# The last store moved behind the branch over the general path, the range check in front of the last sums, and a new order of the work

## The chip, the cores and the metric

The kernel runs on one core of one Trainium2 chip. The metric is the device time of one execution in microseconds (us). TensorE (PE) does the matrix products, VectorE (DVE), ScalarE (ACT) and GpSimd (POOL) the element-wise work, and SyncE (SP) issues nearly all DMAs. Each engine runs its own list of instructions in order and waits on semaphores that the others raise.

## The reference

```python
# q, k, v, a_re, a_im: (batch 4, head 8, seq 768, dim 48)
scale = minimum(mag, 0.999) / (mag + 1e-06)          # mag = |a|
for t in range(S):                                   # complex state S of 48 x 48, per batch and head
    S_re, S_im = a_re_n*S_re - a_im_n*S_im + k_t v_t^T, a_re_n*S_im + a_im_n*S_re
    y[:, :, t] = q_t . S_re
x = y as (4, 768, 384)
h = gelu_tanh(x @ w_in)                              # w_in 384 x 1024
u, v = h[..., :512], h[..., 512:]
v_n = layer_norm(v) * g_ln
v_s = einsum('ts,bsd->btd', w_sg, v_n) + b_sg        # w_sg 768 x 768, along the sequence
out = x + (u * v_s) @ w_out                          # w_out 512 x 384
```

## The kernel before, in words

The program has two paths. The fast path computes the recurrence in chunks of 128 steps by matrix products; it needs the gates (a_re, a_im) and the weights to lie in a range. The general path (`general()`) does the recurrence step by step and is right for any input. The kernel always runs the fast path, gathers on the way the extremes of the gates and weights into `stats`, and at the end branches: if one number, `oki`, says that all 128 partitions were in range, the general path is jumped over; otherwise it runs and writes the output anew. With the inputs timed here it is always jumped over.

The fast path consists of some hundred generators ("chains"), each with a `yield` after every small step: `l`, `g`, `e`, `t`, `p`, `s` (gates: load, logarithms, scale, angles, sine and cosine, by unit of the sequence), `v`, `r`, `z`, `a` (by group of 128 steps: load v, rotate q and k, transpose heads into `Q`, `K` and `kbuf`, attend), `n` (the v half of h, layer norm), `x` (the u half of h), `y` (`spatial()`: v_s, product with u, w_out, sum with x, store), `w` (weights split into a high and a low part, since each product is done as three), `h` and `k` (`gate_range`, `weight_range`), `f` (filler matmuls), `ok` (`check()`). A hand-written string `ORDER` names a chain per token and steps it as often as the token says. A quote mark behind a token sends an element-wise step to POOL or DVE in place of ACT or DVE (`evac`, `high`, `low`, `ew`) and adds filler matmuls in some steps. So the order of instructions on every engine, and in part which engine does a step, is exactly the order of this string.

The end matters here. `y3_0` is the last chain of sums. For its last of four blocks f, PE computes `pvs` (L241), then the products of the first three blocks with w_out (27 matmuls L802 into `po`), while DVE, ACT and POOL make `tg`, `gh` and `gl` of the last block; then come three times three matmuls for the last block (d = 0, 1, 2), each followed by a sum `x<-po,x` on DVE (L832) and a store of 192 KB (L834). The stores of d = 0 and 1 are issued by SP, that of d = 2 by ACT:

```python
(nc.scalar if final and d == NK - 1 else nc.sync).dma_start(out=out[b, ds, tsl], in_=x[:, d, :])
```

The first `ok` step, `in_range()`, stands behind the sums: eight small DVE operations (L844, L845) compare the extremes with their limits, three (L847) multiply the answers, one matmul `pok` (L851) adds them over the partitions, and a cast (L853) writes `oki`. The second `ok` step loads that word into a register of all five engines (TENSOR_LOAD, L964). Then every engine compares and branches (L993). On the path that jumps, each engine raises the semaphores by what the skipped instructions would have raised them: in the built program one step each on ACT, POOL, PE and DVE, and eight in a row on SP, one for each DMA semaphore (named DMAHW0 to DMAHW7 in the program). The end block (L1034) waits on SP for the DMA semaphores, and then all engines meet.

Of the kernel before, what the change touches and what calls it, by code (L numbers as in the profile page):

```python
# [14 lines left out]
ALU = mybir.AluOpType  # L15
# [17 lines left out]
f l0:2 w0 g0:2 g0'' g0:2 w0 g0'' f:2' f f' l1 g1 w0 g0:2 w13 w0 l1 w13:2 t0 m0 e0 w13 w13' w13 p0 g1 e0 p0'' p0:2 s0  # L33
l2 g1:2 e0 g1 w2:3 g1 w2 f m0 e0 e0'' g2 g1:2 w1:4 w1'' w1 e1' l2 s0:2 r0:2'' w6 w6'' v0 t1 p1 g2 e1 g2 p1'' z0' w6'
z0 z0' o0 z0:2 z0' e0 w3 p1 w2'' e0 w3:2 w2 g2 m1 a0 m1 g2 z0 s1 z0' g2 e1:2 e1'' l3 s1:2 e1 t2 g2 p1 g2:4 a0:7 w4 e2
w3 w3'' r1' r1'' v1 w4 l3 m2 o0 w4 e2 w4 g3:2 z1:2 e2 z1 z1' p2 w7 p2' p2 m2 e1 e2'' z1 e2 z1:2 z1' e2:2 a1:2 g3' g3:2
# [4 lines left out]
w5'' z4 v4 n0_0:3 a3 n0_0 z4:5 a4' g5 z4 a4 v5 g5'' r5' z5' z5 g4 z5 w10 w10' a4 p4 m4 z5 m4 w11 a4:3 g5 e4 p4 a4'' p4
l6:2 w10 a4 a4' g5 w14 a4 v6 e4'' e4 n0_0 s4:3 n0_0' z5 z5' z5:2 r6'' w11:2' n0_0 a5' a5 o0 w15 a5:2 n0_0 e4:2 r6 r6'
t5 p5 r6 p5 r6'' n0_0 a5' a5:2 p5 e4 e4' n0_3 g6 x0_0 n0_0 n0_0' x0_0:3 r6 r6'' r6 g5 n0_0'' z6 n0_0'' l8 x0_0 n0_0:2
n0_0' z6 x0_0 z6 x0_0 w15 n0_3 w14 n0_3'' w14 g5 z6 w15 w14 p5 o1 w15 g5 n0_0:2 w14 w14'' n0_3'' g5 n0_3 v7 m5:2 n0_3
x0_0 n0_3 a6 n0_3 a7:2 n0_3:2 a7 w15 w15' p5 a6 n0_3:2 a6:3 a6'' a6 g6 p5 a6'' a6:2 e5 a7'' a7 e5'' n0_3 g6' a6 a7 v8
a7 s5 a7'' a7 e5 n0_3' a6'' e5 a6 a7 n0_3' e5 n0_3 a7 n0_3'' n0_3' n0_3 n0_3'' s5 a7 s5 f r8'' r8 n0_3 n0_3'' g6 x0_3
y0_0 t6 g6 r8'' r8:3 a7 y0_0:3 y0_0' g6 y0_0:2 g6 y0_0 r8 g6:2 p6:3 x0_3:2 y0_0'' x0_3:2 l7:2 x0_3 r8 x0_3 g7:2 y0_0'
# [990 lines left out]
```

## Time and profile before

| | |
|---|---|
| time, median of 3 runs | 434.57 us (433.83 to 434.8) |
| the profiled execution's own time | 435.87 us |
| its span, first to last instruction | 434.2 us, so 1.67 us lie around it |
| mean granted clock of TensorE | 0.992 of full speed |
| busy in the span | PE 96%, DVE 84%, ACT 68%, POOL 29% |
| DMA | 92.95 MB, 214 GB/s |

Busy time is the time in which an engine executes; PE's contains the filler matmuls. The profiled execution is 1.3 us above the median of the runs. A row names a line of the kernel (L241 is line 241), the engine, the operation and the tiles, output first.

### The profile page before, as it was taken

To read this page: it belongs to the slowest core of one execution; us is meant where nothing else is said; L and a number is where in the kernel's file an instruction comes from. 1 tells how busy PE (TensorE), PEld (TensorE's weight loads), DVE (VectorE), ACT (ScalarE), POOL (GpSimd) and SP (SyncE) were. 2 spreads that over 40 slices of the span, in tenths; PEclk is the share of its full clock that TensorE was granted. 3 is DMA by queue.
4 is the path that set the end of the run, shared out by engine and by line. 5 is a ranking of instruction groups with operands and counts; after the bars stand their busy time and mean duration, and the time that the engine had idled before them with its cause. 6 is when DMAs were issued, how large, how long until landed. Compare 5 with 4: busy or idle time off the path is not lost.

```text
span 434.2 us, 9896 instructions
## 1 busy us (share of the span) xinstructions
PE 416.0 (96%) x3924; PEld 378.7 (87%) x3924; DVE 366.8 (84%) x610; ACT 293.2 (68%) x399; POOL 124.1 (29%) x175
## 2 busy tenths in 40 slices
PE   7689999899999999999999999899999999999994
PEld 4367687797999999898999999889999998899994
DVE  5999998998999999988999899887998674768475
ACT  5989999979999497886686862876847223541000
POOL 2047322660602215172112103532131031140010
PEclk9999999989999999999999999999999999999998
DMA  7768675769469988787878985891996956464551
GB/s 222 248 179 246 175 231 136 223 212 286 152 221 246 274 255 258 228 246 231 243 211 253 281 248 166 231 298 47 283 277 226 275 180 200 127 229 125 158 175 59
DMA packets 62940, 92.95 MB, mean 214 GB/s; under 512 B 9892, under 2 KB 44838, under 8 KB 62888
## 3 DMA queue, kind: packets, MB, share of 16 engines
q1 hardware_dynamic: 62744, 92.06, 71.0%
q8 instruction: 32, 0.52, 0.5%
q14 instruction: 20, 0.16, 0.1%
q10 hardware_dynamic: 144, 0.20, 0.1%
HBM read 68.64 MB, written 23.60 MB: 212 GB/s over the span
## 4 chain that ended last, share of the span: by engine, by line
PE 60%; ACT 15%; DVE 12%; DMA 5%; issue 3%; POOL 2%; SPq 1%; DVEq 0%; ACTq 0%
PE pvs L241 20%; PE pu L241 9%; PE pv L241 7%; PE po L802 7%; PE pa L637 5%; ACT L204 4%; PE py L679 3%; PE ps L657 3%; DMA K<-rk 2%; PE py L684 2%; PE pk L622 2%; ACT csn L205 2%; ACT l L205 2%; DMA re<-in_t_re_dram 1%; DVE xl L230 1%
## 5 line engine op out<-in xcount | busy, mean ns | idle before, releaser
L204 ACT ACT_TABLE_LOAD x60 | 77.0, 1283 | 1.9 <-PEq L1023 0.9
L241 PE MATMUL pvs<-wsgh,vh 128*128 128x384 f32 x192 | 65.5, 341 | 0.0
L241 PE MATMUL pvs<-wsgh,vl 128*128 128x384 f32 x192 | 64.7, 337 | 0.0
L241 PE MATMUL pvs<-wsgl,vh 128*128 128x384 f32 x192 | 64.5, 336 | 0.0
L637 PE MATMUL pa<-Q,K 96*64 96x128 f32 (+1 forms) x768 | 40.5, 250 | 1.5 <-DVE K L216 1.4
L637 PEld LDWEIGHTS pa<-Q,K 96*64 96x64 f32 x768 | 36.6, 137 | 5.6 <-issue 3.5
L679 PE MATMUL py<-am,vbuf 128*64 128x128 f32 x384 | 40.4, 281 | 0.1
L241 PEld LDWEIGHTS pvs<-wsgh,vh 128*128 128x128 f32 x192 | 36.0, 188 | 0.6 <-issue 0.4
L241 PEld LDWEIGHTS pvs<-wsgh,vl 128*128 128x128 f32 x192 | 36.0, 188 | 0.3 <-DVE vl L230 0.3
L241 PEld LDWEIGHTS pvs<-wsgl,vh 128*128 128x128 f32 x192 | 36.0, 188 | 0.0
L647 DVE TENSOR_TENSOR am<-pa,mask 128x512 f32<-128x512 f32 x47 | 31.3, 682 | 4.9 <-PE pa L637 4.9
L684 PE MATMUL py<-Q,S 96*48 96x128 f32 x320 | 34.9, 278 | 0.0
L241 PE MATMUL pu<-xh,winh 128*128 128x384 f32 x96 | 33.2, 346 | 0.0
L802 PE MATMUL po<-gh,wouth 128*128 128x384 f32 x96 | 33.0, 343 | 0.0
L241 PE MATMUL pu<-xl,winh 128*128 128x384 f32 x96 | 32.5, 338 | 0.0
L802 PE MATMUL po<-gl,wouth 128*128 128x384 f32 x96 | 32.4, 338 | 0.0
L241 PE MATMUL pu<-xh,winl 128*128 128x384 f32 x96 | 32.4, 337 | 0.0
L802 PE MATMUL po<-gh,woutl 128*128 128x384 f32 x96 | 32.4, 337 | 0.0
L241 PE MATMUL pv<-winh,xh 128*128 128x512 f32 x72 | 29.4, 408 | 0.1
L241 PE MATMUL pv<-winh,xl 128*128 128x512 f32 x72 | 28.6, 398 | 0.9 <-DVE xl L230 0.9
L241 PE MATMUL pv<-winl,xh 128*128 128x512 f32 x72 | 28.4, 394 | 0.0
L679 PEld LDWEIGHTS py<-am,vbuf 128*64 128x64 f32 x384 | 26.5, 138 | 1.5 <-DVE am L647 1.2
(280 smaller groups left out, 1068.3 us busy)
## 6 DMA issues: line engine op xcount, KB each, us to landing
vbuf<-in_t_v_dram SPq DMA_DIRECT2D x24, 288.0 KB, 4.3
K<-rk SPq DMA_DIRECT2D x18, 384.0 KB, 6.2
Q<-rq SPq DMA_DIRECT2D x18, 384.0 KB, 6.4
x<-xd SPq DMA_DIRECT2D x9, 576.0 KB, 4.8
xd<-yp SPq DMA_DIRECT2D x48, 96.0 KB, 3.4
gr<-in_f_im_dram SPq DMA_DIRECT2D x12, 384.0 KB, 4.6
gr<-in_f_re_dram SPq DMA_DIRECT2D x12, 384.0 KB, 4.7
out_dram<-x SPq DMA_DIRECT2D x23, 192.0 KB, 2.5
```

What stands on the lines that cost most here:

```text
L204: nc.scalar.preload_act_table_set(SETS[t])
L205: nc.scalar.activation(out, in_, func, scale=scale, **kw)
L230: ew().tensor_tensor(out=l, in0=src, in1=h.bitcast(F32), op=ALU.subtract)
L241: nc.tensor.matmul(o, w(i), x(i), start=(i == 0 and j == 0), stop=(i == n - 1 and j == 2))
L622: nc.tensor.transpose(pk[:, hh, :], K(4 * g2 + hh), ident[0:2 * D, 0:2 * D])
L637: nc.tensor.matmul(pa[to:to + HC, hh, HC * j:], K(h)[:, HC * j:HC * j + HC], Q(h)[:, HC * j:], start=True, stop=True)
L647: nc.vector.tensor_tensor(out=pairs(am), in0=pairs(pa), in1=upto, op=ALU.mult)
L657: nc.tensor.matmul(ps[r, h, :], kbuf[g % 2][:, h * 2 * D + r.start:h * 2 * D + r.stop], V[:, h * D:(h + 1) * D], start=True, stop=True)
L679: nc.tensor.matmul(py[64 * e:64 * e + 64, p_, :], V[:, at:at + 64], ams[h // 4][:, h % 4, :], start=True, stop=c == 0)
L684: nc.tensor.matmul(py[64 * e:64 * e + D, p_, :], Sb[:, h, :], Q(h), start=False, stop=True)
L802: nc.tensor.matmul(po[d], w[:, f, ds], g[:, f, :], start=f == 0 and j == 0, stop=f == NF - 1 and j == 2)
```

## The change

There are four edits. `ORDER` is written anew as a whole; its last tokens went from `h14:2 y3_0' y3_0 h15 y3_0:8 ok y3_0 ok` to `h14:2 y3_0 y3_3:2 ok y3_0:7 f:2 ok`, so the first `ok` step now comes before the last sums and the second one at the very end. The last of the three sums goes to a tile of its own, `end`, with the tag "u", whose buffers the general path uses as well. Its store is taken out of `spatial()` and stands in `last_store()`, behind the branch. It is still issued by ACT. Line numbers behind the sums shift by 6 to 10: the check is L850 to L859, the load L973, the branch L1002, the last store L968, the end block L1044.

```diff
 ORDER = """
-f l0:2 w0 g0:2 g0'' g0:2 w0 g0'' f:2' f f' l1 g1 w0 g0:2 w13 w0 l1 w13:2 t0 m0 e0 w13 w13' w13 p0 g1 e0 p0'' p0:2 s0
+l0 o0 l0 g0 w0 g0:4 l1 w13 l1 g1 m0 w0:2 g0'' w0 f'' g0:2 w13 o0 w13:2 w13'' w13' t0 e0 g1 e0 m0 p0 p0'' p0:2 s0 g1''
...
 """
@@ spatial
             result(d, range(NF - 1, NF) if final else range(NF))
             yield
+            if final and d == NK - 1:
+                if "end" not in run:
+                    run["end"] = mp.tile([P, MT], F32, tag="u", name="end", bufs=UB)
+                nc.vector.tensor_tensor(out=run["end"], in0=po[d], in1=x[:, d, :], op=ALU.add)
+                yield
+                return
             nc.vector.tensor_tensor(out=x[:, d, :], in0=po[d], in1=x[:, d, :], op=ALU.add)
             yield
-            (nc.scalar if final and d == NK - 1 else nc.sync).dma_start(out=out[b, ds, tsl], in_=x[:, d, :])
+            nc.sync.dma_start(out=out[b, ds, tsl], in_=x[:, d, :])
             yield
@@
+    def last_store():
+        nc.scalar.dma_start(out=out[B - 1, DM - P:DM, UFINAL * P:UFINAL * P + MT], in_=run["end"])
+
@@
     with tc.If(ok[0] < P, label="over"):
         general()
+    last_store()
```

By the order of the built programs PE keeps its 2756 matmuls on the fast path, fillers included. DVE goes from 607 to 595 instructions, ACT from 395 to 399 and POOL from 179 to 184; ACT's table loads go from 60 to 59.

The first place is ACT's list up to `xh` of the block n0_3, the high part of x that the first layer-norm block of the second half of the sequence needs. `yp` is the evacuated attention output, `vr` the normalized v, `inv`, `re` and `l` belong to the gates. Before:

```order
L218 COPY yp<-py 128x512 [waits DMAHW4_49,DMAHW5_49,DMAHW3_49,DMAHW6_49,DVE_49,PE_49]
L204 ACT_TABLE_LOAD
L205 ACTIVATE re_1005<-re_1005 128x768 [waits DMAHW2_49]
L204 ACT_TABLE_LOAD
L205 ACTIVATE u__1181<-pu 128x384 [waits PE_49]
L205 ACTIVATE u__1194<-pu 128x384 [waits PE_49]
L205 ACTIVATE vr<-vr,nt,ny 128x512 [waits DVE_49,Pool_49]
L205 ACTIVATE vh_1217<-vr 128x512 [waits Activation_49]
L205 ACTIVATE vr<-vr,nt,ny 128x512 [waits DVE_49]
L205 ACTIVATE u__1224<-pu 128x384 [waits PE_49]
L205 ACTIVATE xh<-x 128x1152 [waits DMAHW6_49,DMAHW7_49,DMAHW5_49,PE_49]
```

After:

```order
L218 COPY yp<-py 128x512 [waits DMAHW5_49,DMAHW6_49,DVE_49,PE_49]
L204 ACT_TABLE_LOAD
L205 ACTIVATE inv_852<-l_971,cols 128x768 [waits DVE_49]
L205 ACTIVATE re_914<-re_914 128x768 [waits DMAHW1_49]
L204 ACT_TABLE_LOAD
L205 ACTIVATE u__1184<-pu 128x384 [waits PE_49]
L205 ACTIVATE u__1201<-pu 128x384 [waits PE_49]
L205 ACTIVATE vr<-vr,nt,ny 128x512 [waits Pool_49]
L205 ACTIVATE u__1214<-pu 128x384 [waits PE_49]
L205 ACTIVATE vh_1216<-vr 128x512 [waits Activation_49]
L205 ACTIVATE xh<-x 128x1152 [waits DMAHW5_49,DMAHW6_49,DMAHW4_49,PE_49]
```

`inv<-l,cols` has come in front of `xh`, and the second `vr<-vr,nt,ny` has gone behind it.

The second place is the end of DVE's list, where `ok_...` holds the answers of the check and `stats` the extremes. Before, the three sums, then the check:

```order
L395 ISA stats 128x1
L832 TENSOR_TENSOR x<-po,x 128x384 [waits PE_49] x3
L844 TENSOR_REDUCE ok_5176<-stats 128x1
L845 TENSOR_SCALAR ok_5176<-ok_5176 128x1 [waits DVE_49]
L844 TENSOR_REDUCE ok_5176<-stats 128x1
```

After, the end of the check, the cast, and then the sums:

```order
L853 TENSOR_TENSOR ok_5163<-ok_5163 128x1
L853 TENSOR_TENSOR ok_5163<-ok_5163 128x1 [waits DVE_49] x2
L855 MEMSET ones 128x2
L859 CAST oki<-pok 1x2 [waits PE_49]
L838 TENSOR_TENSOR x<-po,x 128x384
L838 TENSOR_TENSOR x<-po,x 128x384 [waits PE_49]
L835 TENSOR_TENSOR end<-po,x 128x384 [waits PE_49]
L973 TENSOR_LOAD oki [waits DVE_49]
L1002 COMPARE_AND_BRANCH
```

The whole check has moved in front of the sums, and between the last sum and the branch only the load is left. On PE, `pok` has moved the same way: it now stands between the matmuls of d = 0 and those of d = 1.

The third place is ACT's end. Before, with the store in front of the load and the branch (the row behind them belongs to the skipped path):

```order
L205 ACTIVATE gh<-tg 128x384 [waits DVE_49,PE_49]
L834 DMA out_dram<-x 128x384 [waits DMAHW5_49,DVE_49]
L964 TENSOR_LOAD oki [waits DVE_49]
L993 COMPARE_AND_BRANCH
L205 ACTIVATE winh<-bits 128x512 [waits DVE_49] x5
```

After, the rows at the end of the skipped path, and the store behind it:

```order
L205 ACTIVATE gh<-tg 128x384 [waits DVE_49] x4
L1002 UNCONDITIONAL_BRANCH
L1002 UNCONDITIONAL_BRANCH [waits Activation_49]
L968 DMA out_dram<-end 128x384 [waits DMAHW7_49,DVE_49]
L1044 UNCONDITIONAL_BRANCH
```

The store now waits for a DMA semaphore, DMAHW7, and for DVE. In the built program the counts it waits for contain what the skipped path would have added: they are reached by the last of SP's eight steps behind the branch and by DVE's step.

## Rows read from the trace of the kernel before

**Rows 1.** Windows: length, busy of PE, PEld, DVE, ACT, POOL; clock, DMA share, GB/s.

```profile
80.00:102.00 22.00, 19.88 (x160) 17.31 (x159) 19.79 (x31) 19.72 (x24) 11.93 (x18) 0.92 0.75 227
102.00:420.00 318.00, 316.40 (x3057) 302.67 (x3058) 268.72 (x441) 200.59 (x271) 83.88 (x107) 1.00 0.74 221
```

**Rows 2.** Waits of PE, 30 to 430 us: total, times, longest.

```profile
PE pa L637 <- DVE K L216: 1.4, 1, 1.4
PE pk L622 <- DMA K<-rk: 1.2, 1, 1.2
```

**Rows 3.** Chain of waits, 80 to 104 us: start, length, what.

```profile
84.04 1.91 DVE k L467
...
86.77 0.58 DVE K L216
...
92.27 0.59 ACT yp L218
```

**Rows 4.** ACT by line and shape, 0 to 104 us: count, busy, mean ns.

```profile
L218 ACT COPY K<-pk 96x512 f32<-96x512 f32 x10 | 5.8, 576 | 0.0
...
L218 ACT COPY Q<-pk 96x512 f32<-96x512 f32 x6 | 3.4, 573 | 0.0
...
L205 ACT ACTIVATE inv<-l,cols 128x768 f32<-128x768 f32 x2 | 1.9, 932 | 0.0
...
L205 ACT ACTIVATE vr<-vr,nt,ny 128x512 f32<-128x512 f32 x2 | 1.6, 809 | 0.0
L205 ACT ACTIVATE vh<-vr 128x512 fp32r<-128x512 f32 x2 | 1.3, 626 | 0.0
```

**Rows 5.** DVE by line and shape, whole span: count, busy, mean ns.

```profile
L467 DVE TENSOR_TENSOR k<-k,em 128x768 f32<-128x768 f32 x9 | 9.6, 1067 | 0.5 <-ACT em L205 0.5
```

**Rows 6.** POOL from 76 to 96 us: start, length, what.

```profile
82.18 2.95 POOL L230 TENSOR_TENSOR wsgl<-raw,wsgh 128x768 fp32r<-128x768 f32 x1
```

**Rows 7.** Timeline from 427 us, all engines: start, length, what.

```profile
427.31 1.61 DVE L832 TENSOR_TENSOR x<-po,x 128x384 f32<-128x384 f32 x3 [1.06 <-PE po L802]
...
427.89 0.87 SPq L834 DMA_DIRECT2D out_dram<-x  x2
...
428.83 0.15 DVE L844 TENSOR_REDUCE ok<-stats 128x1 f32<-128x12 f32 x1
...
430.48 0.19 PE L851 MATMUL pok<-ones,ok 128*1 128x2 f32 x2 [2.15 <-DVE ones L849]
430.70 0.15 DVE L853 CAST oki<-pok 1x2 int32<-1x2 f32 x1 [0.28 <-PE pok L851]
```

**Rows 8.** Line 964, the load of the word to branch on: ns, start.

```profile
L964 SPq TENSOR_LOAD <-oki x1: 467/467/467, 430.9 to 430.9; - x1
```

**Rows 9.** Line 993, the branch: ns, first and last start.

```profile
L993 SPq EVENT_SEMAPHORE  x8: 17/17/17, 432.2 to 432.8; - x8
...
L993 SPq COMPARE_BRANCH  x1: 70/70/70, 431.7 to 431.7; - x1
...
L993 DVEq EVENT_SEMAPHORE  x1: 21/21/21, 432.1 to 432.1; - x1
```

**Rows 10.** Line 1034, the end of the program: ns, first and last start.

```profile
L1034 SPq EVENT_SEMAPHORE  x10: 17/28/28, 432.9 to 434.1; - x10
...
L1034 SPq DRAIN  x3: 7/7/7, 433.4 to 433.7; - x3
```

**Rows 11.** Line 834, all stores of sums: issue to landing.

```profile
DMA to landing us min/median/max: 1.9/2.5/5.5
```

**Rows 12.** Timeline of DVE, 422 to 427 us: start, length, what.

```profile
422.68 0.56 DVE L818 TENSOR_TENSOR tg<-u__4962,tg 128x384 f32<-128x384 f32 x1
...
423.64 1.25 DVE L395 CUSTOM_DVE_ANT_0 gr<-gr 128x768 f32<-128x768 f32 x1
```

**Rows 13.** Page, part 6: KB, median us from issue to landing.

```profile
K<-rk SPq DMA_DIRECT2D x18, 384.0 KB, 6.2
...
gr<-in_f_im_dram SPq DMA_DIRECT2D x12, 384.0 KB, 4.6
```

More of the change, by code (lines that the diff above doesn't have):

```diff
@@ L43 @@
[L43 to L47, printed above, removed]
@@ L78 @@
-y3_3 h20 x3_0:5 h20 h10 h10' y3_3:5 k1:2 y3_3:3 h3 h3' k6 y3_0:2 y3_0'' y3_0 y3_3 h15 y3_0'' y3_0:2 y3_0'' h9 h9'
-y3_0' k6 y3_0' y3_0:3 y3_0' y3_0'' y3_0:6 k0:2 h14:2 y3_0' y3_0 h15 y3_0:8 ok y3_0 ok
+l0 o0 l0 g0 w0 g0:4 l1 w13 l1 g1 m0 w0:2 g0'' w0 f'' g0:2 w13 o0 w13:2 w13'' w13' t0 e0 g1 e0 m0 p0 p0'' p0:2 s0 g1''
+l2 e0 g1:2 g2 e0 g1' w2:3 w1 g1 w2 g1 s0 e0 w1:3 v1 e1'' w1'' l2 s0 r0 r0'' z0'' t1 w6 p1 w6'' g2 g2'' z0:3 p1' e0 z0
+l3 e1 a0 z0' w3 w6' m1 p1 e1 z0' z0'' w2' w2 p1 w1 g2 e1 o1 m1 o0 w3 e1'' g2 s1:3 v0 w3 t2 g2:5 e0 g2 g3 a0:2 a0'' a0
@@ new lines @@
+e3 n0_0 z4 n0_0:2 z4 l6 n0_0 g4 e3 v5 w5' w5 a4 a3 a4'' z4 z4' z5' r5'' g5 z4 g5'' p4 z5 w10 a4 g5 z5:2 g4 w10' g5
+a4'' p4 m4 w10 m4 p4 w11 w11:2' a4 e4 e4'' e4 w14 a4 a4'' a4 s4:2 a4'' v6 s4 n0_0:2 a4 z5 z5'' z5:2 r6 n0_0 t5 a5 a5''
+a5 a5'' a5' a5 n0_0 e4'' e4:2 g5 w15 r6 r6' n0_0 r6 a5 r6'' e4'' n0_3 g5 r6 r6'' r6 p5:3 g6 n0_0 n0_0'' x0_0:3 f:2
+n0_0 w14 x0_0 f x0_0 n0_0' x0_0 n0_0 x0_0 n0_3 n0_0 x0_0 w14 n0_3 w14 n0_0'' w14 w15 n0_3'' n0_0 g5 w15 n0_0'' w14''
+n0_3 z6:4 w15 g5 w15 w15' n0_3:2 a7 n0_3 p5:2 n0_3 v7 a7 n0_3:3 a6:2 n0_3 a6 l6 a6:2 a6'' g6 a7 a6 m5:2 p5 a6:2 a7' a6
@@ new lines @@
+g6' e5 a7 e5 a6 a7:2 a7'' a7:2 e5 a6'' a7'' a7 s5 o1 e5'' e5 a6 s5:2 r8 n0_3:2' n0_3:2'' l7 n0_3 n0_3'' r8 n0_3' x0_3
+n0_3:2 r8'' y0_0 g6 t6 g6 l7 y0_0 r8:2 y0_0'' y0_0 g6 y0_0' r8 y0_0:2 g7 g6 z8 x0_3 r8'' g6 y0_0'' x0_3:2 a7 y0_0 g6
+x0_3 r8 v9 p6 x0_3:2 m6 p6:2 g7 g7'' p6 y0_0'' g7 z8:2 p6 y0_0:3 y0_0' y0_0'' y0_0:2 y0_0'' g7 m6 a8 y0_0' z8 a9 y0_3
+g7 a7 e6 a8' a8 v8 e6:2 s6:3 l8 y0_0'' a9 g7 l8 y0_3 r10'' g8 l9 r10 y0_0 a8 e5 a8 r10'' r10 t7 e6:2 a8:2 r10' y0_0
+e5' a8'' y0_0 a8:2 g7 r10 r10'' r10 g7 a8'' a8:2 a9 y0_0 m7 y0_0:2 a9 p7:2 a8 g9 e7 e7' y0_0:2 a9 p7:2 a9'' a9 e7 a9:3
@@ new lines @@
+a9' a9 p7 y0_3'' m7 g8 p7 y0_3'' y0_0 y0_3 g8'' x0_3 z10:2 e6 y0_3:2 z10 e7'' s7 y0_3'' z10 s7 y0_3'' v10 y0_3'' a9 e7
+v11 a9 s7 g8 t8 n1_0 r12'' r12 a10 r12' r12 a10 y0_3 e6' a10 r12:2 a10 g8 a10 a10'' a10 a10'' a10 y0_3 l9 n1_0 a10
+y0_3'' y0_3 y0_3' a10:4 r12 g8:2 a11:3 y0_3 a11 p8 m8 g8 a11:2 n1_0 p8 e7:2 y0_3 p8 y0_3' g9 g9'' p8:2 y0_3:2 n1_0
+g9:3 n1_0 z12 r12 a11 p8 n1_3 n1_0 g8 n1_0:5 g9 a12 a13 n1_0 v12 l10 n1_3' l10 a12 y0_3 n1_3 y0_3 n1_0 z12:3 y0_3:4
+v13 s8 y0_3:2 m8 y0_3 e8 a13'' e8'' e8 g9 s8 g9 s8 x1_3 t9 x1_3 n1_0:2' n1_0'' n1_0' n1_0:2 n1_0' n1_0'' n1_0' n1_3:7
@@ new lines @@
+g10:3 g11 x1_0 z16:4 p10:3 m10 y1_3' a15 v17 g11 g11'' e10 a15 e10:2 y1_3' g11 y1_3:3 e10' y1_3 a16 y1_3:5 a16'' a16
+a16' a16 a16'' a16 a16'' s10:2 a16 t11 a16:2 s10 a16:2 p11 a17 h8 r18'' h8 e10 g11 p11 a17:2 p11 y1_0 h1 a17'' a17
+y1_0 r18 h6 e10 r18'' n2_0 r18 a16 r18' g11 n2_0 r18:3 e10'' p11 n2_0'' g11 p11 s11 h16 a17'' a17 p11 s11:2 y1_0
+y1_0:2' y1_0:2 h23 m11 y1_0'' y1_0 y1_0' y1_0:2 y1_0'' y1_0 n2_0 z18 h1'' g11 y1_0' n2_3 y1_0:2 g11 y1_0:3'' n2_0:6
+a19 n2_0:2 h19 e11 z18:2 y1_0 e11'' n2_3' m11 n2_3' y1_0 e11 a18 y1_0:2 h23 x2_3:2 r20 y1_0 n2_0:2 r20 z18 v18 y1_0
@@ new lines @@
+a19 r20'' e11'' h6 n2_0:2 l12 n2_0' l12 r20 n2_0:3 n2_0'' n2_0' n2_3:3 x2_3 n2_3 h19 k11 n2_3 x2_3 e11 v19 a18''
+n2_3:3 x2_3 r20'' a19 r20 x2_3 n2_3 a18 y1_0 r20:2 a19 a18'' e11 y1_0:2 e11'' a18 a18'' a18:3 m12 a18 a19 a18 a19''
+a19:5 a18 n2_3 n2_3'' n2_3 n2_3' n2_3'' n2_3 a18 n2_3'' x2_0 a19 a19'' n2_3'' n2_3 h16 n2_3' a19 k11 g12 z20 g12:2
+y2_3:2 y2_3'' y2_3' x2_3 x2_0 x2_0'' g12 x2_3 t12 g12 v21 y2_3:3 y2_3:2'' y2_3' k8 h7 y2_3:4 y2_3'' y2_3 g12 z20 y2_3
+v20 y2_3' z20:2 a21 p12:2 a21'' x2_0 m12 y2_3'' p12 y2_0 g12 p12 g12 a20 k2 x2_0 y2_3'' y2_0 a21 k2 a20 h22 g12 e12
@@ L80 @@
+n3_3' k7 n3_3 n3_3'' k7 n3_3 n3_3'' n3_3 n3_3'' k12 x3_3 k9 x3_3:3 x3_0 h15:2 x3_0' x3_0'' h17 y3_3:2 y3_3:2' y3_3''
+y3_3:2 y3_3:3'' f y3_3 h12:2 y3_3 y3_3:3'' f:2 y3_3:2 x3_0 y3_3'' y3_3:2' f x3_0 h2 h2' k1 x3_0 k1 x3_0:2 k0 h4:2 h17
+f:2 k0 y3_3:2 x3_0 y3_3:2 x3_0:2 h13 y3_3 f y3_3 k5 y3_0:2 k5 y3_3 y3_0' k4 h9 k4 y3_0 y3_0' h13 y3_0:2 y3_0' y3_0
+y3_0'' h20 h3 h20 h3 y3_0:4 k6:2 y3_0 h9 y3_0 f y3_0:4 y3_0:2'' y3_0' h14:2 y3_0 y3_3:2 ok y3_0:7 f:2 ok
 """
```

54 lines of the change are left out of this document (15 added, 39 removed).

## The prediction

> **What bounds the kernel now.** I read three views in this order. First the windows: from 102 to 420 us PE is busy for 316.40 of 318.00 us, while DVE and ACT have slack of 49 and 117 us [rows 1]. The change keeps all of PE's matmuls, so in this stretch no order of the others can give more than the 1.6 us that PE idles. Before 102 us it is otherwise: from 80 to 102 us DVE and ACT are busy for 19.79 and 19.72 of 22 us, PE's clock is 0.92 there, and PE's busy time includes fillers [rows 1]. So the front is bound by ACT and DVE and the middle by PE. Second, PE's waits: behind 30 us the long ones are 1.4 us for a copy of K by DVE and 1.2 us for the load K<-rk [rows 2]. The chain of waits shows what the first costs: DVE's k and K end at 87.35, PE's attention matmuls follow, and ACT can evacuate yp only at 92.27 [rows 3]. Third, the timeline of the tail: the sums begin at 427.31, right behind PE, and end at 428.92. Everything from there to 434.2 is 5.3 us in which PE does only the small product pok, and in which check, load, branch and end stand in a row [rows 7 to 10]. This is what the change rebuilds.
>
> **Front, step by step.** Up to the `xh` of n0_3 ACT has 126 instructions before and 125 after. Counted by kind over the two lists, `inv<-l,cols` is one more (0.932 us), `winh` one more (no such row on ACT up to here; the row of `vh`, of the same shape, 0.626), and `vr<-vr,nt,ny`, a copy K and a copy Q one less each (0.809, 0.576, 0.573) [rows 4]. That is 1.558 - 1.958 = -0.40 us. The bounds: nothing, if the chain through DVE's K and PE sets the time there, since ACT waits for py in that place [rows 3]; and -0.8 if the removed vr alone counts and inv hides in the wait for DVE. I take -0.4, since ACT is nearly full in that window. DVE's list up to the xl behind it is one instruction shorter, from which I take nothing.
>
> **Middle.** Over the whole fast path the kinds that move are mostly DVE's that go to POOL (some products with em, ep and cosine; subtractions of vl) and to ACT (copies of kbuf and yp). DVE's list is 12 instructions shorter. Since DVE has slack behind 102 us, I cost this at 0; its cover is PE's 99.5%. If a piece that PE needs gets late on the slower POOL, it costs PE that delay. The wait for K<-rk I leave as it is: its median from issue to landing is 6.2 us [rows 13], and in the new order the first K load of that unit again stands behind a burst of other loads, so the wait moves rather than goes. Bounds: -1.2 us (it goes) and +1.2 (a second one).
>
> [...] The row first: DVE's `k<-k,em` at 84.04 takes 1.91 us [rows 3], where its kind has a mean of 1.067 [rows 5]; beside it POOL subtracts `wsgl` from 82.18 to 85.13 [rows 6]. So a meeting of the two costs DVE some 0.9 us, and here it sits in the chain to K. [...] In the middle this changes nothing, since DVE has slack; in front one meeting more in the chain to K would be +0.9, one less -0.9.
>
> **Tail, step by step.** Before: the last sum ends at 428.92, the first comparison begins at 428.83, pok at 430.48, the cast ends at 430.85 [rows 7]; SP's load begins at 430.9 [rows 8]; its branch ends at 431.77, its eight semaphore steps run from 432.2 to 432.8 [rows 9]; its end list runs from 432.9 and the first drain comes at 433.4 [rows 10]; the span ends at 434.2, 0.8 later.
> After: the 1.65 us from the first comparison to pok [rows 7] lie beside PE's matmuls, if they are done when d = 0 is. DVE ends the last product tg at 423.24 [rows 12]; then come a cast of the same tile (not among the rows; at the most that product's 0.56, which reads two inputs), a gate range (1.25 [rows 12]), a sum (a third of 1.61, 0.54 [rows 7]) and the check: 423.24 + 0.56 + 1.25 + 0.54 + 1.65 = 427.24. PE ends d = 0 at about 427.3, where the sums began. So pok waits for nothing, but with a margin of less than 0.1.
> In front of the sums DVE now waits for pok and the cast: from 430.48 to 430.85, 0.37. The sums run from 427.68 to 429.29. The second one ends at 428.75; SP needs half of 0.87 [rows 7] to issue its store and stands at the load at 429.2, in place of 430.9. From load to the end of the branch 0.87: 430.1. Gap 0.43: 430.5. Eight steps 0.6: 431.1. They include the wait for the second store, which lands 1.9 to 2.5 us after its issue [rows 11]: 430.65 to 431.25, so it costs next to nothing.
> So far that is 1.7 us earlier. But what was behind it, the end list, now has to wait for the last store, which was long issued before. It stands on ACT behind a semaphore that SP's eighth step completes, so it goes at 431.1, though its data have been there since 429.3. It lands at the least 1.9 later [rows 11]: 433.0. One step and 0.8 of drains and barrier: 433.9, against 434.2. **Tail -0.3.** Bounds: if the store needs only DVE's step, which came 0.7 before SP's last [rows 9], -1.0; if it lands at the median of 2.5, +0.3. I take 1.9, since nothing else moves in the DMA queues then.
> [...]
>
> **Sum.** -0.4 - 0.3 = -0.7 us. The profiled execution took 435.87 us, 1.3 above the median of the runs; the differences are worked out in it and set against the median: 434.57 - 0.7 = 433.9 us.
>
> **Rivals.** (1) The middle and the front shorten more than their sum: the wait for K of 1.4 and that of 1.2 go [rows 2], and so does the low clock. From 80 to 102 us a mean clock of 0.92 over 22 us is 1.8 us of full-speed work lost [rows 1]; a PE that doesn't wait for K before it may keep its clock. All of it gives 433.9 - 4.4 = 429.5, half of it 431.7. For it speaks that DVE has less to do, against it that the same kinds of DVE work stand ahead of K in the new order, and that some fillers in front of these matmuls are gone.
> (2) The other side: a new wait in the front. The order is new everywhere, and ACT and DVE are full there. One late operand that holds PE and lets the clock fall costs what the old one did, 1.4 + 1.8 = 3.2, less the 0.7: 437.1; a load as late as K<-rk, 1.2, gives 435.1. It decides from 1.6 us on.
> (3) The check holds PE. The gate range in front of it needs a load of 384 KB that now comes right in front of its use, and such loads take 4.6 us in the median [rows 13]. Each us beyond that margin stops PE's last six matmuls, and all behind them. With 0.6 late: 433.9 + 0.6 = 434.5.
> (4) The tail gives nothing: the store lands at 2.5 or the instructions behind the branch come late, +0.6 to +1.2: 434.5 to 435.1.
>
> **How the numbers follow.** 0.2% is 0.87 us, which is about what a measurement of this kernel can tell: faster is below 433.70, slower above 435.44. The forecast as summed gets 0.42, with its own range from 433.0 to 434.9, a third of it below 433.70. Rival (1) gets 0.28, all faster. Rivals (3) and (4) together get 0.14, nearly all of it within 0.2%. Rival (2) gets 0.16, mostly slower. So faster 0.14 + 0.28 = 0.42, same 0.28 + 0.10 = 0.38, slower 0.04 + 0.16 = 0.20. The range of 8 in 10 leaves out the far half of (1) and of (2): 430.9 to 436.5.
>
> **What would show it.** Right: PE's row of pok without idle time in front of it; the sums about 0.4 later behind d = 0's matmuls; SP's load 1.7 earlier against the last matmul, 0.8 behind the end of the second store's issue; the last store issued by ACT within 0.1 of SP's eighth step; the end list waiting for it; from the last sum to the end of the span 4.6 to 4.9 us in place of 5.3. In front, the `xh` of n0_3 0.4 earlier than before. The prediction falls if the low clock around 90 us goes or comes again elsewhere, if PE's waits behind 30 us differ from the sum of before by over 1 us, or if the last store issues before SP's eight steps.

## The result, and the profile after

The changed kernel takes 441.17 us (median of 6 runs, 437.92 to 443.37) and the kernel before, on the same chip, 434.54 (6 runs, 433.83 to 435.98). The ratio is 1.0143, with a 95% interval of 1.0103 to 1.0183: slower. The forecast of 433.9 and its range up to 436.5 were wrong.

The profiled execution took 441.46 us. The head of its page (times with the share of the span, and instructions):

```profile
span 439.7 us, 9883 instructions
...
PE 418.3 (95%) x3924; PEld 379.8 (86%) x3924; DVE 359.6 (82%) x598; ACT 294.3 (67%) x404; POOL 143.4 (33%) x180
```

The span has grown by 5.5 us, from 434.2 to 439.7. Three marks in the two traces, all of them starts, say where. The `xh` of n0_3 starts at 101.44 instead of 99.55 (+1.9); the first `pvs` matmul at 120.73 instead of 118.56 (0.3 more); the last matmul of the sums at 432.51 instead of 427.99 (2.35 more); and from there to the end of the span it is 7.15 instead of 6.17 (+1.0). So front, middle and end have all lost.

The windows that answer to [rows 1], with one more for the low clock (length, busy of PE, PEld, DVE, ACT, POOL; clock, DMA share, GB/s):

```profile
85.70:92.50 6.80, 6.70 (x50) 5.10 (x52) 5.71 (x11) 4.81 (x6) 1.95 (x2) 0.50 0.60 181
80.00:102.00 22.00, 19.73 (x161) 16.77 (x158) 19.30 (x30) 17.79 (x23) 10.69 (x11) 0.84 0.55 172
102.00:420.00 318.00, 314.44 (x3039) 299.37 (x3038) 261.51 (x429) 201.32 (x273) 98.53 (x110) 1.00 0.73 221
```

From 85.7 to 92.5 us the granted clock is 0.50. Before, it was at 0.50 only from 89.4 to 92.8. These 3.4 us more at half speed are 1.7 us of full-speed work, which would account for nearly all that `xh` has lost. From 102 to 420 us PE idles for 3.56 us, where it was 1.60. The waits behind 30 us, which answer to [rows 2] (total, times, longest):

```profile
PE pk L594 <- DVE S L666: 1.9, 1, 1.9
PE pv L241 <- DVE xl L230: 1.3, 2, 0.7
PE py L679 <- DVE am L647: 1.0, 1, 1.0
PE pvs L241 <- POOL vl L230: 1.0, 1, 1.0
PE pu L241 <- ACT u__2846 L205: 0.8, 1, 0.8
PE pa L637 <- ACT Q L218: 0.7, 1, 0.7
```

Both waits of [rows 2] are gone, for DVE's K and for K<-rk. Four others stand in their place: 1.9 us for S in the front, and 1.0, 0.8 and 1.0 for am, u and vl at 157, 229 and 307 us. The list differs from one execution to the next: in another one of the changed kernel (after_again below) PE waits 0.3 for S and 1.6 for yp behind it, and not for vl.

**Why S is late.** POOL's and DVE's timelines around it (start, length, what):

```profile
80.55 1.21 POOL L225 TENSOR_SCALAR wsgh<-raw 128x768 fp32r<-128x768 f32 x1 [3.40 <-DMA raw<-in_moe_w_sg_dram]
81.85 2.41 POOL L230 TENSOR_TENSOR wsgl<-raw,wsgh 128x768 fp32r<-128x768 f32 x1
...
81.00 1.57 DVE L230 TENSOR_TENSOR wsgl<-raw,wsgh 128x768 fp32r<-128x768 f32 x1
82.49 1.79 DVE L524 COPY left<-csn 128x3 f32<-128x3 f32 x1
84.20 0.94 DVE L467 TENSOR_TENSOR k<-k,em 128x768 f32<-128x768 f32 x1
85.07 0.54 DVE L666 TENSOR_TENSOR S<-ps,S 96x384 f32<-96x384 f32 x1
```

`left` is a copy of three columns; before it took 0.15 us. Here it takes 1.79 and ends at 84.28, just as POOL's `wsgl` does (81.85 + 2.41 = 84.26). The row above it has the same look: DVE's `wsgl` starts at 81.00, POOL's `wsgh` ends at 81.76, and DVE ends 0.81 after that, at 1.57 us in place of 0.94. POOL's side is longer too: its `wsgl` takes 2.41, where the shortest of the four on POOL in this kernel takes 1.82. So in these rows each of the two engines seems to hold the other up. S stands two rows behind `left`; PE has nothing to do from 83.7 on and goes on at 85.67.

The starts don't tell which of the two has to wait. In the kernel before, POOL's `wsgl` runs from 82.18 to 85.13 [rows 6], and these rows of DVE's timeline start inside it:

```profile
82.43 0.15 DVE L524 COPY left<-csn 128x3 f32<-128x3 f32 x1
82.50 0.94 DVE L230 TENSOR_TENSOR wsgl<-raw,wsgh 128x768 fp32r<-128x768 f32 x1
```

They take no longer than in after_w11_dve below (0.16 and 0.94). There it was POOL's `wsgl` that took 2.95, and only the `k` of [rows 3] was held. In after_again POOL's `wsgl` runs from 84.11 to 86.58 and holds another row:

```profile
83.25 0.80 DVE L524 COPY left<-csn 128x3 f32<-128x3 f32 x1
...
85.40 1.60 DVE L669 TENSOR_TENSOR S<-S,dec 96x384 f32<-96x384 f32 x1
```

Six profiled executions have the new front with POOL's `wsgl` in this place. In two of them (after, new_order_store_first) `left` takes 1.79 us; in the four others it takes 0.79 or 0.80, and `S<-S,dec` 1.59 to 1.63 in place of 0.55. In the four where the step is moved or on DVE, `left` takes 0.15 or 0.16.

What makes one of the two wait, no run here shows; the rows show only that it happens while both run, and for how long.

**The middle.** The wait for am at 157 us shows the same, and that for vl shows the other side (DVE's row first, then POOL's):

```profile
154.68 2.30 DVE L512 TENSOR_TENSOR_SCAN im<-im 128x256 f32<-128x256 f32 x1
...
154.62 1.81 POOL L467 TENSOR_TENSOR k<-k,em 128x768 f32<-128x768 f32 x1 [6.64 <-DMA k<-in_u_k_dram]
...
302.15 1.30 POOL L230 TENSOR_TENSOR vl<-vr,vh 128x512 fp32r<-128x512 f32 x1 [4.26 <-ACT vh L205]
304.89 2.67 POOL L230 TENSOR_TENSOR vl<-vr,vh 128x512 fp32r<-128x512 f32 x1 [1.44 <-ACT vh L205]
```

The scan, 0.63 us each for the two in front of it, takes 2.30 beside POOL's product, which ends at 156.43; am stands behind it. The second `vl` takes 2.67 instead of 1.30 while DVE runs the range scans of gates and weights (L395 and L327, 304.99 to 306.41); in after_again it takes 1.31. The wait for u is ACT's order: from 221.9 to 229.1 it has three table loads of 1.28 us and four activations of the gates in front of that u.

**The end.** The rows that answer to [rows 7], from the timeline:

```profile
431.40 0.19 PE L857 MATMUL pok<-ones,ok 128*1 128x2 f32 x2
...
431.63 0.15 DVE L859 CAST oki<-pok 1x2 int32<-1x2 f32 x1 [0.94 <-PE pok L857]
431.71 1.21 DVE L838 TENSOR_TENSOR x<-po,x 128x384 f32<-128x384 f32 x2
...
432.27 1.01 SPq L840 DMA_DIRECT2D out_dram<-x  x2
...
432.88 0.56 DVE L835 TENSOR_TENSOR end<-po,x 128x384 f32<-128x384 f32 x1
436.87 0.38 ACTq L968 DMA_DIRECT2D out_dram<-end  x1
```

SP's rows of the branch, to [rows 9], and of the load, to [rows 8] (ns, first and last start):

```profile
L973 SPq TENSOR_LOAD <-oki x1: 469/469/469, 433.3 to 433.3; - x1
...
L1002 SPq EVENT_SEMAPHORE  x8: 17/17/17, 434.7 to 436.8; - x8
...
L1002 SPq COMPARE_BRANCH  x1: 70/70/70, 434.2 to 434.2; - x1
```

The load has moved up as meant: 0.8 us behind the last matmul instead of 2.9. But SP's eight steps take 2.1 us instead of 0.6, and the last store goes out with the eighth, at 436.87. The fifth step comes at 436.56. It is the one that waits for the second store, as the DMA part for 432.9 to 436.6 shows (queue: packets, MB, share; then issues, KB each, us to landing):

```profile
q1 hardware_dynamic: 288, 0.39, 31.8%
q14 instruction: 4, 0.03, 2.6%
q8 instruction: 1, 0.02, 2.1%
...
out_dram<-x SPq DMA_DIRECT2D x1, 192.0 KB, 3.6
```

That store, issued at 432.95, lands 3.6 us later, where the least of [rows 11] was 1.9. In the same stretch the trace has five packets with instructions, which start at 433.87 to 435.25 and take 0.3 to 1.3 us each. Before, the same five came at 432.5 to 432.8, when all stores had landed, and the stretch of its stores, 428.4 to 430.6, shows none:

```profile
q1 hardware_dynamic: 288, 0.39, 49.4%
q10 hardware_dynamic: 144, 0.20, 23.5%
```

In both traces these packets come behind the first branches, those of ACT, POOL and PE: these start at 432.3 to 432.4, and the first packet at 433.87; before, at 431.4 to 431.5 and 432.51. That the branch is what brings them is my reading of this order; no run shows it.

How the late store's data came shows in the same part for two stretches, up to 434.6 and from there to 436.5:

```profile
q1 hardware_dynamic: 268, 0.37, 63.1%
...
q1 hardware_dynamic: 20, 0.03, 5.4%
```

So 268 of the 288 packets of the two stores had moved by 434.6. The last 20 came nearly one by one up to 436.1, and the two latest packets with instructions (434.97 and 435.25) ran among them.

### The profile page after: what moved, and what is told of

The parts are those of the page before. It is cut to its first block, busy times and chain, and to the rows that moved or that the text cites. A ratio compares the mean times of both kernels' runs of the same rounds, so it can differ in the third digit from the quotient of the medians.

```text
span 439.7 us, 9883 instructions
## 1 busy us (share of the span) xinstructions
PE 418.3 (95%) x3924; PEld 379.8 (86%) x3924; DVE 359.6 (82%) x598; ACT 294.3 (67%) x404; POOL 143.4 (33%) x180
## 4 chain that ended last, share of the span: by engine, by line
PE 72%; ACT 15%; DVE 6%; issue 3%; DMA 1%; POOL 1%; SPq 0%; DVEq 0%; ACTq 0%
PE pvs L241 18%; PE po L802 12%; PE pv L241 11%; PE pu L241 8%; PE pa L637 6%; ACT L204 5%; PE py L679 4%; PE py L684 3%; PE ps L657 2%; PE pk L622 2%; ACT vr L205 2%; ACT csn L205 2%; DMA re<-in_t_re_dram 1%; ACT inv L205 1%; PE pk L594 1%
## 5 line engine op out<-in xcount | busy, mean ns | idle before, releaser
L815 DVE SCALAR_TENSOR_TENSOR tg<-pvs,gcol,bsg 128x384 f32<-128x384 f32 x32 | 19.6, 612 | 17.0 <-PE pvs L241 15.0
```

What stands on the lines that cost most here:

```text
L815: nc.vector.scalar_tensor_tensor(out=tg, in0=pv, scalar=gcol[:, f:f + 1], in1=bsg[:, tsl], op0=ALU.mult, op1=ALU.add)
```

## The experiments

My theory after the result: the loss has three parts, each with its own cause. In the front and middle, POOL's and DVE's turns hold DVE where PE waits, and PE's idling in front is followed by a longer fall of the clock; at the end, the last store stands in series with the branch. The rivals: the order as a whole is worse for reasons spread over it, or the order is harmless and the end alone costs it all.

The table gives each kernel's ratio to the kernel before on the same chip with its 95% interval; the other columns are from its one profiled execution: the last matmul of the sums, from there to the end of the span, and the time at half clock up to 140 us. Before had 427.99, 6.17 and 3.4 there, after 432.51, 7.15 and 6.8. In seven kernels (new_order_old_tail, new_order_store_first, old_front_new_rest, after_pool_back, before_w11_late, old_order_new_end, after_again) 3.4 us of the last column lie at 13 to 14 us, far ahead of the waits named here.

| kernel | ratio | last matmul | to the end | half clock |
|---|---|---|---|---|
| new_order_old_tail | 1.0067 [1.0035, 1.0099] | 432.26 | 6.17 | 6.8 |
| new_order_store_first | 1.0101 [1.0063, 1.0139] | 435.87 | 5.83 | 10.2 |
| new_front_old_rest | 1.0043 [1.0012, 1.0074] | 433.21 | 6.17 | 10.2 |
| old_front_new_rest | 1.0198 [1.0160, 1.0236] | 437.86 | 6.17 | 10.2 |
| after_w11_late | 1.0300 [1.0254, 1.0346] | 438.17 | 6.94 | 10.2 |
| after_pool_back | 1.0287 [1.0242, 1.0331] | 439.98 | 7.32 | 13.6 |
| before_w11_late | 1.0268 [1.0226, 1.0310] | 441.21 | 6.16 | 17.1 |
| after_fill | 1.0092 [1.0064, 1.0120] | 429.63 | 7.18 | 0 |
| after_w11_dve | 1.0076 [1.0047, 1.0105] | 428.31 | 7.06 | 0 |
| after_all_back | 1.0029 [1.0000, 1.0058] | 430.41 | 6.17 | 0 |
| before_fill | 0.9993 [0.9962, 1.0024] | 426.78 | 6.17 | 0 |
| before_pool | 1.0006 [0.9976, 1.0037] | 428.12 | 6.17 | 0 |
| old_order_new_end | 1.0044 [1.0015, 1.0073] | 428.96 | 7.03 | 3.4 |
| old_order_early_check | 1.0023 [0.9989, 1.0056] | 428.13 | 5.69 | 0 |
| after_again | 1.0102 [1.0054, 1.0150] | 431.02 | 6.87 | 6.8 |

### The order and the end apart

**new_order_old_tail**: the new order, with sums, check and store as before.

```diff
-h14:2 y3_0 y3_3:2 ok y3_0:7 f:2 ok
+h14:2 y3_0 y3_3:2 y3_0:7 ok y3_0 ok
```

> The new order as it is, but the end as before: the check behind the sums, the last store issued by ACT in front of the branch. Theory: of the 5.5 us between the two profiled spans 4.5 lie ahead of the last matmul (1.9 up to 102 us, 2.6 between) and 1.0 behind it; so this kernel takes about 1.0 less than the changed one, 440.2 us, and from its last matmul to the end 6.2 us as before. Rival: the new end is what costs, and the order only shifts waits around; then it takes about 434.5 to 435.5.

**new_order_store_first**: the new order with the early check, and the store in front of the branch.

```diff
-h14:2 y3_0 y3_3:2 ok y3_0:7 f:2 ok
+h14:2 y3_0 y3_3:2 ok y3_0:8 ok
...
-    last_store()
```

> The new order with the check in front of the sums, but the last store issued by ACT in front of the branch, from x, as before. Theory: the loss of the new end is that the last store stands behind the landing of the second one (1.9 in series); without it the early check gives its gain: from the last matmul to the end about 5.5 us (7.2 in the changed kernel, 6.2 before), so 1.7 below the changed kernel, 439.5 us. Rival: the instruction packets that the branch brings in delay all three stores just as much, and the stretch stays at 6.5 to 7.2.

The order alone costs 0.67%, 2.9 us, and its end is back at 6.17. With the early check and the store in front of the branch the end is 5.83 in the profile: the check's new place gives 0.3, and it is the store's place behind the branch that takes 1.3 (7.15 - 5.83). In time the 0.3 isn't shown: the ratio of that second kernel is no lower, and the two intervals overlap. Its profiled execution had 10.2 us at half clock, which may be why. So "the end costs it all" doesn't hold. That the order doesn't cost it all either rests on old_order_new_end below, where the new end alone costs 0.44%.

**new_front_old_rest** and **old_front_new_rest**: the two orders cut near 100 us and joined crosswise, with the old end. A cut order isn't half of either: steps that one half has done already fall out of the other.

```diff
-n0_0' z6 x0_0 z6 x0_0 w15 n0_3 w14 n0_3'' w14 g5 z6 w15 w14 p5 o1 w15 g5 n0_0:2 w14 w14'' n0_3'' g5 n0_3 v7 m5:2 n0_3
+n0_0' z6 x0_0 z6 x0_0 w15 n0_3 w14 n0_3'' g5 x0_0 w14:3 n0_3'' n0_0 g5 w15 n0_0'' w14'' n0_3 z6 w15 g5 w15 w15' n0_3:2
```

(This is the joint of old_front_new_rest.)

> The new order up to the xl of n0_3 (about 102 us), behind it the steps that are left in the old order, with the old end. Theory: the front alone is 1.9 us later (PE waits for S at 86 us, then has half the clock up to 92), and the rest, bound by PE, keeps that: 436.4 us. Rival: the front's delay is made up behind it, 434.5.

> The old order up to the xl of n0_3, behind it the steps that are left in the new order, with the old end. Theory: the waits of PE behind 102 us (am 1.0 at 157, u 0.8 at 229, vl from POOL 1.0 at 307 us) cost 2.6 more than before: 437.1 us. Rival: these waits are themselves a result of the late front, so they go with it: 434.5 to 435.5.

These don't tell the shares apart. Each joint brought a wait that neither order has: 2.4 us for K<-rk at 109 us in the first, 3.7 us for a u of ACT at 130 us in the second, and each was followed by 6.8 us at half clock. What they show, in one execution each, is how an operand late by a few us costs twice, by the wait and by the clock behind it.

### The turns of POOL and DVE in the front

**after_w11_late**: the step that meets `left`, moved behind the third step of n0_3. **before_w11_late** does the same to the kernel before, and **after_pool_back** adds to the first that two middle steps go from POOL back to DVE.

```diff
-w11 w11:2' a4
+w11 a4
...
-n0_3 w14 n0_0''
+n0_3 w11:2' w14 n0_0''
```

```diff
-a8 g9 e7 e7' y0_0:2
+a8 g9 e7:2 y0_0:2
...
-h16 n2_3' a19
+h16 n2_3 a19
```

> The changed kernel with one edit: the split of one w_sg block on POOL (wsgh, then wsgl, 3.6 us beside DVE's wsgl and the copy left, which took 1.57 and 1.79 us there in place of 0.94 and 0.15) moved behind the xl of n0_3. Theory: POOL's two-input operation stretches DVE's, so S and K come late; without it left takes 0.15 again, PE's wait for S of 1.9 shrinks below 0.5, and the clock falls for 3.4 us or not at all in place of 6.8: 1.7 to 3.4 us less than the changed kernel. Rival: the long left is a wait for something else on DVE (the granted order), and neither it nor the wait changes.

> The kernel before with the same step of POOL moved behind the xl of n0_3. Theory: DVE's k<-k,em at 84 us takes 1.07 in place of 1.91, K is 0.9 earlier, PE's wait of 1.4 shrinks to 0.5, and 0.9 us are won, up to 2.6 if the clock no longer falls. Rival: K waits for DVE's other work, nothing won.

> The kernel of the run before this one, with two more steps given back from POOL to DVE: the k<-k,em that began at 154.6 us, beside which DVE's scan took 2.30 in place of 0.63, and the last vl of n2_3, which took 2.67 on POOL in place of 1.30. Theory: PE's waits for am (1.0 at 157 us) and for vl (1.0 at 307 us) go, another 2.0 us less. Rival: DVE is then later by what it takes over (1.07 and 0.68), and PE waits there for something else as long.

All three missed by far, in both orders. The wait for S is gone, but a larger one has come; PE's waits and SP's of after_w11_late:

```profile
PE pv L241 <- ACT xh L205: 9.5, 1, 9.5
...
SPq L269 <- POOL wsgl L230: 12.5, 1, 12.5
```

SP's next load goes into the buffer that `wsgl` has to read first. It waits for it, from the store of xd at 83.55 to 96.95, and everything queued behind it on SP waits as well, the stores of xd and the load of x among them. I had moved a step with slack on POOL and not looked at the queue that it releases. In the middle, after_pool_back did to the waits what it should: am's fell from 1.1 to 0.4 and vl's went. But the stretch from the first `pvs` to the last matmul is 311.43 us with it and 311.39 without, and the ratios are 1.0287 and 1.0300. So that the two waits cost as much as they last isn't shown.

**after_w11_dve**: the place kept, but the second half of `wsgl` also on DVE.

```diff
-w11 w11:2' a4
+w11 w11' w11 a4
```

> The changed kernel, only the wsgl of that w_sg block on DVE in place of POOL, so no transfer's place changes. Theory: DVE has one operation more (0.94) but wsgl and left beside it take 0.94 and 0.15 in place of 1.57 and 1.79, so S comes about 1.3 earlier, PE's wait for S of 1.9 falls to about 0.6, the clock falls for 3.4 us or not at all: 1.3 to 3 us less than the changed kernel. Rival: the wait stays at 1.5 or more, since DVE only trades one operation for the other.

Rows of its DVE timeline, and its window from 84 to 94 us:

```profile
82.10 0.16 DVE L524 COPY left<-csn 128x3 f32<-128x3 f32 x1
82.17 0.94 DVE L230 TENSOR_TENSOR wsgl<-raw,wsgh 128x768 fp32r<-128x768 f32 x1
83.04 0.94 DVE L467 TENSOR_TENSOR k<-k,em 128x768 f32<-128x768 f32 x1
83.91 0.54 DVE L666 TENSOR_TENSOR S<-ps,S 96x384 f32<-96x384 f32 x1
...
84.00:94.00 10.00, 8.60 (x101) 7.38 (x102) 9.90 (x18) 8.56 (x11) 5.52 (x6) 1.00 0.70 219
```

`left` is back at 0.16 although DVE has one more operation, and S comes 1.16 us earlier. So the meeting with POOL held it, as the theory says. PE still waits 1.2 for S, but the clock stays at 1.00 (the same window after: 0.66), and `xh` comes at 98.23 instead of 101.44. The ratio falls from 1.0143 and 1.0102, in the two batches of the changed kernel, to 1.0076; that is clear of noise against the first batch and not against the second.

**after_fill**: nothing moved, but three filler matmuls added to PE's list around there.

```diff
-s4 n0_0:2 a4
+s4 n0_0 n0_0'' a4
```

> The changed kernel with three filler matmuls (1 us of work) in front of the last pv matmuls of n0_0, so that PE's idle time before S is about 0.9 in place of 1.9 us. Theory: the clock falls because of that idle time, so it keeps full speed or falls for 3.4 us in place of 6.8, and the time is 1.7 to 3.4 us lower while S is as late as before. Rival: the clock falls for the idle times further ahead (69, 76 us) all the same, and nothing changes.

In its profile the clock didn't fall either (1.00 from 84 to 94 us), and the last matmul came at 429.63. The timed ratio of 1.0092 is lower than the changed kernel's by less than the intervals, so that a filler alone repairs it isn't settled.

**after_all_back**: the new order with the old end, `wsgl` on DVE, the filler, and the two middle steps back on DVE.

```diff
-w11 w11:2' a4
+w11 w11' w11 a4
...
-s4 n0_0:2 a4
+s4 n0_0 n0_0'' a4
...
-a8 g9 e7 e7' y0_0:2
+a8 g9 e7:2 y0_0:2
...
-h16 n2_3' a19
+h16 n2_3 a19
...
-h14:2 y3_0 y3_3:2 ok y3_0:7 f:2 ok
+h14:2 y3_0 y3_3:2 y3_0:7 ok y3_0 ok
```

> The new order with the old end and all the repairs together: wsgl, the k<-k,em of 154.6 us and the last vl of n2_3 back on DVE, and three fillers more in front of the last pv of n0_0. Theory: what the order loses is these waits and the clock, so the last matmul comes within 1 us of where it was before, and the time is that of the kernel before, 0.995 to 1.003 of it. Rival: the order loses in other places as well, and 1.005 or more is left.

1.0029 [1.0000, 1.0058], against 1.0067 without the repairs. From the first `pvs` to the last matmul it is 309.78 us, against 309.43 before and 311.78 after. What is left are waits of 1.0 for K<-rk, twice 0.5 for am, and 0.8 for u. The time is in the theory's range, but the last matmul comes 2.4 us later than before, not within 1; 2.1 of that lie ahead of the first `pvs` (120.63 against 118.56), although the clock didn't fall (1.00 from 84 to 94 us). The two intervals overlap, so how much of the order's loss the named meetings carry isn't settled; the last 0.3% lies at the edge of the measurement.

### The same places in the old order

**before_pool** sends two steps of the middle from DVE to POOL in the kernel before; **before_fill** gives its wait for K a filler.

```diff
-z10:3 e7 v10
+z10:3 e7' v10
...
-e11' n2_3'' r20:2
+e11' n2_3' r20:2
```

```diff
-a5' a5 o0 w15 a5:2 n0_0
+a5' a5 o0 w15 a5'' a5 n0_0
```

> The kernel before with the two steps that the new order gives to POOL put there (the k<-k,em near 158 us and the last vl of n2_3), nothing else. Theory: the operations of DVE beside them take up to twice as long, and PE waits there for 0.5 to 1 us each: 1.001 to 1.005 of the time before. Rival: DVE has slack there, the waits don't appear, 1.000; then it is the neighbourhood in the new order and not the choice of the engine that costs.

> The kernel before with three filler matmuls (1 us) in front of the second half of the attention scores of group 5, in the place where PE waits 1.4 us for K. Theory: the clock falls at 89 us because of that idle time; without it py takes half as long and the xh of n0_3 comes 1.5 to 2 us earlier: 0.996 of the time before. Rival: the clock falls anyway, nothing won.

before_pool is no slower. POOL meets DVE there too: `S<-S,dec` takes 2.20 us beside the one step and 1.25 beside the other, in place of 0.55 and 0.56.

```profile
156.83 2.20 DVE L669 TENSOR_TENSOR S<-S,dec 96x384 f32<-96x384 f32 x1
```

But PE waits for neither. So it isn't POOL's slower product that costs (2.17 us for `k<-k,em`, on DVE 0.95), nor the meeting by itself, but who on PE waits for the row that is held. It shows something else: the wait for K of 1.4 us is there as in [rows 2], but in this execution no fall of the clock follows, and none follows it in those of old_front_new_rest, old_order_new_end and old_order_early_check. The fall that [rows 1] show was the exception among five. before_fill removes that wait and has the shortest profiled span, 432.9, but timed it is the same as before: no gain that can be measured.

### The end alone

**old_order_new_end** and **old_order_early_check** keep the old order up to the last line; the first has the whole new end, the second the early check with the store in front of the branch. **after_again** is the changed kernel on their chip.

```diff
-h15 y3_0:8 ok y3_0 ok
+h15 y3_0 ok y3_0:7 ok
```

```diff
-h15 y3_0:8 ok y3_0 ok
+h15 y3_0 ok y3_0:8 ok
```

> The old order with the new end: check in front of the last sums, the last store behind the branch. The old order has one gate range more in front of the check, so pok comes about 0.6 late and PE stops for that. Theory: the second store lands 3.4 to 3.6 us after its issue in place of 1.9, since the instruction packets after the branch meet it, and the last store follows its landing: from the last matmul to the end 7.1 us in place of 6.2, and with the 0.6 the kernel takes 1.004 of the time before. Rival (my prediction's sum): the second store lands in 1.9, the stretch is 5.9, 1.001.

> As the run before this one, but the last store is issued by ACT in front of the branch. Theory: stores land late for the packets, but only once in a row: 5.8 us from the last matmul to the end, 0.4 less than before, which pok's 0.6 takes back: 1.000 to 1.001. Rival: 6.5 and more, 1.002.

> The changed kernel unaltered, on the chip of these two. Theory: the order costs what the old order with the new end does not: 1.008 to 1.014 of the time before, with the end's 0.002 in it. Rival: the two orders differ by less than 0.3% and the end is the most of it: 1.003 to 1.006.

SP's steps and its branch in old_order_new_end, and the steps in old_order_early_check:

```profile
L1002 SPq EVENT_SEMAPHORE  x8: 17/17/17, 431.2 to 433.1; - x8
...
L1002 SPq COMPARE_BRANCH  x1: 70/70/70, 430.6 to 430.6; - x1
```

```profile
L993 SPq EVENT_SEMAPHORE  x8: 17/17/17, 430.3 to 432.5; - x8
```

In both the steps take about 2 us, and the fifth comes 3.5 and 3.3 us behind the issue of the second store (after_again: 3.3). With the store behind the branch the end is 7.03, with it in front 5.69: 1.3 apart, as in the new order. Timed, the new end costs 0.44% in the old order, 1.9 us with an interval from 0.7 to 3.2; the traces give 0.86 for the end and 0.54 for `pok`, which in this order waits for the check. The early check alone has 0.48 less at the end, pays the same 0.54, and times the same as before.

## Why the prediction was wrong, step by step

**Tail: the mechanism was right and one term mis-sized.** `pok` has no wait in front of it but 0.25 us of issue, the cast delays the first sum by 0.2 and the last not at all (0.4 was worked out), the load comes right behind the second store, load to branch takes 0.9, the last store issues within 0.1 of SP's eighth step, lands 1.9 later, and the span ends 0.8 after the drains: nearly all as worked out. The failed step is "They include the wait for the second store, which lands 1.9 to 2.5 us after its issue [...] so it costs next to nothing". It landed after 3.6, the eight steps took 2.1 instead of 0.6, and the tail is +1.0 instead of -0.3. That is rival (4), a little above the +0.6 to +1.2 that it added to the forecast. Of the last store I had said that "nothing else moves in the DMA queues then"; beside the second one, five packets with instructions moved. The last store, with none of them beside it, took 1.9 again, the one beside the instruction packets 3.6. That the packets make it late is shown only as a coincidence: in all nine executions whose branch comes before that store has landed, it takes 3.3 to 3.8 us. No run took the packets away.

**Middle: the failed step is "In the middle this changes nothing, since DVE has slack".** Slack over 318 us said nothing about single places. Twice a step on POOL met one on DVE, once ACT's order was late, and PE waited 1.0, 1.0 and 0.8. Of the 2.35 us by which the stretch from the first `pvs` to the last matmul grew, PE's idle time makes 1.45 (2.90 in place of 1.45); what the rest is, no run shows. That the middle did lose shows in all executions together: that stretch is 308.2 to 310.2 us in the seven with the old order there, 309.8 to 313.7 in the nine with the new one. Which waits carry the loss isn't shown as firmly: vl's is missing in after_again, and taking two of them away shortened nothing in after_pool_back. The wait for K<-rk, of which I wrote "the wait moves rather than goes", is absent in this execution; but it is 0.3 to 1.6 us in others of the old order and 1.0 in after_all_back, so this pair of executions doesn't decide it.

**Front: the failed step is the -0.40 from counting ACT's instructions, with DVE's list put at nothing ("from which I take nothing").** In kernels of the new order without a fall of the clock, `xh` comes at 98.17 (after_fill), 98.23 (after_w11_dve) and 99.51 (after_all_back), in old ones at 98.38 to 99.35 (old_order_early_check, before_fill, before_pool), so the shortening isn't shown. What set the time in the changed kernel was DVE's chain to S, which the count of ACT didn't see. I had the row for it, POOL's `wsgl` beside DVE's `k` [rows 6, 3], priced a meeting at 0.9 and said "one meeting more in the chain to K would be +0.9"; it then met `left`, in the chain to S, for 1.64 us, and the clock was low for twice as long. That is rival (2) in kind, which I gave 0.16; its 437.1 is 4 us short, since it had one wait in the front and nothing for the middle and the end. The rows show what a meeting can cost: `left`, 0.15 us in the kernel before, took 1.79 and ended 0.02 behind POOL's `wsgl`; the scan of 0.63 took 2.30.

**What stays open.** How much of the timed 1.0143 the clock takes differs by execution: the six runs have mean clocks of 0.983 to 0.991, and the slowest of them the lowest clock. The two batches of the changed kernel, 1.0143 and 1.0102, overlap. Which of POOL and DVE waits when they meet, and why the meeting falls on another row in another execution, no run decides. The rest of after_all_back isn't explained by an experiment. No kernel here beats the one before by more than can be measured.

## What to carry to other kernels

Before a step moves between DVE and POOL, lay the two timelines side by side where it will stand: it was not its own length that counted here but what of the other engine ran beside it, and who on PE waited for that (`left` with 1.79 us: 1.9 of PE's time in the changed kernel; `S<-S,dec` with 2.20: none in before_pool). The meeting fell on a neighbouring row in the next execution (`left` 1.79 us in one, `S<-S,dec` 1.60 in after_again), so one trace isn't enough. The transfer placed behind the branch waited here for everything that the branch's semaphore steps waited for (the fifth of SP's steps came at 436.56, with the second store's landing, and the last store at 436.87), so the earlier branch brought that store no gain here while the one in front of it had not landed. And a step with slack on its own engine may still release a buffer for which a whole DMA queue waits (12.5 us in after_w11_late).

## What the runs showed of the hardware that I had not expected

- A DVE operation beside one of POOL was held until about POOL's end: in the changed kernel a 128x3 copy took 1.79 us instead of 0.15 and ended 0.02 after it, a scan of 0.63 took 2.30 and ended 0.55 after it. The other way round POOL's 1.30 became 2.67 beside DVE's range scans. The starts don't tell who is held: in the kernel before, the same copy began 0.25 us after POOL's `wsgl` and took 0.15.
- Five instruction packets of 0.3 to 1.3 us each came behind the branches. In the nine executions where the second store of 192 KB had not landed by then, it took 3.3 to 3.8 us from its issue to its landing (3.6 in the changed kernel), and 1.9 in the kernel before and in new_order_old_tail, where it had landed ahead of them.
- After the same idle time of 1.4 us in front of PE's attention matmuls the clock fell to half for 3.4 us in one execution (the kernel before) and not in four others (before_pool, old_front_new_rest, old_order_new_end, old_order_early_check).
- One POOL step that ended 13 to 15 us later cost 9.5 to 11.7 us of PE's time (9.5 in after_w11_late, 9.6 in after_pool_back, 11.7 in before_w11_late), through a buffer that SP's queue waited for.
